# Two column pairs of the MLP's first product as 2x2x2 blocks of seven products

## The chip, the cores and the metric

The kernel runs on one core of one Trainium2 chip. The metric is the device time of one launch in microseconds (us), the median of several runs. TensorE is PE in the profile, with its weight loads as PEld; VectorE is DVE, ScalarE is ACT, GpSimd is POOL. SyncE (SP) issues most of the DMAs.

## What is computed

The reference is one transformer-like block on x of 2048 tokens by 512 channels, all in float32: a linear attention, then an MLP across the token axis.

```python
h = x + _A_ref(_layernorm(x, axis=-1), A_wqkv, A_w_phi, A_wo)
h2 = h + _B_ref(_layernorm(h, axis=-1), B_w1, B_b1, B_w2, B_b2)
```

Only the second line matters for the change. `_B_ref` normalizes its input once more and computes

```python
u = jnp.einsum("bsd,sf->bdf", h, w1) + b1                  # (B, D, F)
u = _gelu(u)
y = jnp.einsum("bdf,fs->bds", u, w2) + b2                  # (B, D, S)
```

with S = 2048, D = 512 and F = 1792. The first product multiplies W1 (2048 x 1792, transposed) with the normalized h (2048 x 512); the second multiplies W2 with the result u.

## The kernel before

**Three matmuls for one.** TensorE works in the type `float32r`. Every operand is split into a high part, a rounded copy, and a low part, the rest: the helper `split` (L56 to L59) has ACT write the high part and DVE or POOL subtract it. A product is then hi x hi + hi x lo + lo x hi: three matmuls (`mm3`, L61 to L65), added up in PSUM.

**The attention stage** ends at about 263 us. In it every engine's order is written out by hand (`tc.manual_schedule`, closed at L709). For each of the 16 token tiles t it forms h (`s_h`, L570), writes it to the output tensor `out` (L575), computes its mean and reciprocal deviation r2 (`s_moments`, `s_rstd`) and the normalized h, split into the tile `HN[t]` of 128 x 2 x 512 (`s_hn`, L587: two ACT operations, then the split with POOL as the subtracting engine). The 16 tiles HN stay in SBUF in the pool `big`, which has 18 places.

**The first product** (from L763) runs over seven column pairs p of W1, each 2 x 128 columns. For a pair, `fill` (L629) goes over the 16 token tiles: each time two blocks of 128 x 128 weights against the whole HN[t], 512 columns wide, three matmuls each, into two PSUM banks. W1 comes in chunks of two token tiles (`stream`, L612): one DMA of 256 KB on SP, an ACT copy to whi (L603), a DVE subtraction to wlo (L610); the pool `wf` holds four chunks. Pairs 0 and 1 run for the most part inside the attention stage, where TensorE has room for them; pairs 2 to 6 follow. After a pair, ACT applies the gelu from PSUM into a tile `u` (L738, pool `ur`, four places).

**The second product** already works in blocks of seven products. Take two operands as 2 x 2 blocks; seven products of sums of blocks (Winograd's form) take the place of eight. `operands_u` (L741) forms the block sums of u, with four subtractions of 128 x 256 by POOL for pairs 0 and 1 and by DVE for pairs 2 to 6, and splits all seven. Pairs 0 and 1 go to tiles of their own (`near`), pairs 2 to 6 into places of `big` that HN leaves. `stream_w2` (L779) loads blocks of W2 (two steps at a time, 256 KB each), sums them in four DVE operations (L789 to L792) and splits them; `products` (L803) issues the 7 x 3 = 21 matmuls of a step, 256 columns wide (L801). There are 8 row pairs with 7 steps each. At the end of a row pair `e`, `u2` and `u3` put the seven results together, and the rows are added to `out` by an accumulating DMA.

**The order.** After L709 a planner in the compiler orders the instructions of each engine: by the order in which the program issues them, by what is ready in its own timing model, and with pools handing out places as they come free. On the chip each engine then goes through its list in order. `tc.issue_after(x)` keeps what is issued inside it behind the instruction x on its engine; W2's sums use it, with an entry of `LO`, the list of W1's wlo subtractions.

Of the kernel before, what the change touches and what calls it, by code (L numbers as in the profile page):

```python
# [9 lines left out]
F32 = mybir.dt.float32  # L10
F32R = mybir.dt.float32r
AF = mybir.ActivationFunctionType
# [5 lines left out]
P = 128  # L18
S, D, H, DH, F = 2048, 512, 32, 16, 1792
NT = S // P  # L20
# [14 lines left out]
def block_kernel(ctx: ExitStack, tc: tile.TileContext, x, xT, wT, phic, wo, w1, b1, w2, b2,  # L35
                 kvmask, ident_in, out):
    nc = tc.nc

    cst = ctx.enter_context(tc.tile_pool(name="cst", bufs=1))
# [11 lines left out]
    cst.tile([P, 80], F32, name="pad")  # L51
# [4 lines left out]
    def split(hi, lo, src, lo_engine):  # L56

        nc.scalar.activation(hi, src, AF.Copy)  # L58
        lo_engine.tensor_sub(lo, src, hi)  # L59
# [452 lines left out]
    wst = ExitStack()  # L512
# [5 lines left out]
    HN, HT, PHT, OS, PO, VE = {}, {}, {}, {}, {}, {}  # L518
# [68 lines left out]
    def s_hn(t):  # L587
        hn = ak.tile([P, D], F32, name="hn")
        nc.scalar.activation(VE[t][:, 1:2], VE[t][:, 1:2], AF.Copy, scale=r2[:, t:t + 1])
        nc.scalar.activation(hn, HT[t], AF.Identity, scale=r2[:, t:t + 1], bias=VE[t][:, 1:2])  # L590
        HN[t] = big.tile([P, 2, D], F32R, name="hs", tag="big")
        split(HN[t][:, 0], HN[t][:, 1], hn, nc.gpsimd)
# [128 lines left out]

    NP = NF // 2
    HD = D // 2
    up = ctx.enter_context(tc.tile_pool(name="up", bufs=1, side="right", reuse_waits="tile"))
    uo = ctx.enter_context(tc.tile_pool(name="uo", bufs=2, side="right", reuse_waits="tile"))
    ws = ctx.enter_context(tc.tile_pool(name="ws", bufs=2, side="right", reuse_waits="tile"))
    ur = ctx.enter_context(tc.tile_pool(name="ur", bufs=4, side="right", reuse_waits="tile"))
    ut = ctx.enter_context(tc.tile_pool(name="ut", bufs=1, side="right", reuse_waits="tile"))
    ps_b = ctx.enter_context(tc.tile_pool(name="ps_b", bufs=4, space=PSUM, reuse_waits="tile"))
    NEAR = 2  # L730
    near = [up.tile([P, 7, 2, HD], F32R, name=f"un{p}") for p in range(NEAR)]
    up.tile([P, 120], F32, name="pad")
    U, UB, far = {}, {}, {}

    def gelu(f, pu):
        if f % 2 == 0:
            U[f // 2] = ur.tile([P, 4, HD], F32, name="u")
        nc.scalar.activation(U[f // 2][:, f % 2 * 2:f % 2 * 2 + 2].rearrange("p k d -> p (k d)"), pu,  # L738
                             AF.Gelu_apprx_tanh, bias=b1s[:, f:f + 1])

    def operands_u(p):  # L741
        u = U[p]
        tt = ut.tile([P, 3, HD], F32, name="tt")
        e = nc.gpsimd if p < NEAR else nc.vector
        e.tensor_sub(tt[:, 0], u[:, 0], u[:, 1])
        e.tensor_sub(u[:, 0], u[:, 2], u[:, 0])
        e.tensor_sub(tt[:, 1], u[:, 2], tt[:, 0])
        e.tensor_sub(tt[:, 2], u[:, 3], tt[:, 1])
        if p < NEAR:
            for n0, src in ((0, u), (4, tt)):  # L750
                o = near[p][:, n0:n0 + src.shape[1]]
                split(o[:, :, 0], o[:, :, 1], src, nc.vector)
            for m in range(7):
                UB[p, m] = near[p][:, m]
            return
        for m in range(7):
            at = (p - NEAR) * 7 + m
# [5 lines left out]
    for p in range(NP):  # L763
        while FN[p] < NT:
            fill(p, ps_b)
        for c in range(2):
            gelu(2 * p + c, PU[p][c])
        if p < NEAR:
            operands_u(p)
    for p in range(NEAR, NP):  # L770
        operands_u(p)
# [7 lines left out]
    def stream_w2(n):  # L779
        steps = STEPS[n:n + GRP]  # L780
        raw = ws.tile([P, GRP, 7, P], F32, name="wraw", bufs=3)
        wh_ = ws.tile([P, GRP, 7, P], F32R, name="whi")
        wl_ = ws.tile([P, GRP, 7, P], F32R, name="wlo")
        for i, (sp, p) in enumerate(steps):
            nc.sync.dma_start(raw[:, i, 0:4].rearrange("p (k i) s -> p k (i s)", k=2),
                              w2v[:, 2 * p:2 * p + 2, sp * 2 * P:(sp + 1) * 2 * P])
            AW[sp, p] = wh_[:, i], wl_[:, i]
        with tc.issue_after(LO[-18]):
            nc.vector.tensor_add(raw[:, :, 4], raw[:, :, 0], raw[:, :, 2])  # L789
            nc.vector.tensor_sub(raw[:, :, 0], raw[:, :, 1], raw[:, :, 0])  # L790
            nc.vector.tensor_sub(raw[:, :, 5], raw[:, :, 4], raw[:, :, 1])
            nc.vector.tensor_sub(raw[:, :, 6], raw[:, :, 3], raw[:, :, 5])  # L792
        split(wh_, wl_, raw, nc.vector)


    PROD = ((1, 1, 0, 0, True), (2, 6, 2, 1, True), (3, 3, 3, 1, True), (4, 4, 2, 0, False), (0, 0, 1, 0, True),
            (5, 5, 0, 1, False), (6, 2, 3, 0, False))

    def product(o, a, b, start, stop):
        for i, (x, y) in enumerate(((0, 0), (0, 1), (1, 0))):  # L800
            nc.tensor.matmul(o, a[x], b[:, y], start=start and i == 0, stop=stop and i == 2, skip_group_check=True)  # L801

    def products(sp, ps, order):  # L803
        for a, b, bk, half, opens in order:
            for p in ps:
                wh_, wl_ = AW[sp, p]
                product(bank[bk][:, half], (wh_[:, a], wl_[:, a]), UB[p, b], p == 0 and opens, p == NP - 1)

    def flat(a):
        return a.rearrange("p k d -> p (k d)")  # L810

    for n, (sp, p) in enumerate(STEPS):
# [4 lines left out]
        if p == 0:  # L817
            pools = [ps_f, ps_f, ps_q, ps_q] if sp % 2 else [ps_b] * 4
            bank = [pool.tile([P, 2, HD], F32, name="py", tag="pu") for pool in pools]
        if p < NP - 1 - 2 * last:  # L820
            products(sp, [p], PROD)
            continue
# [3 lines left out]
        e = uo.tile([P, 2, HD], F32, name="e")  # L826
        u2 = uo.tile([P, HD], F32, name="u2", bufs=1)
        u3 = uo.tile([P, HD], F32, name="u3")
        if not last:
            products(sp, [p], by_bank)  # L830
            ot = uo.tile([P, 2, 2, HD], F32, name="ot", bufs=1)
            nc.scalar.activation(e[:, 1], bank[0][:, 0], AF.Copy)
            nc.vector.tensor_add(u2, bank[0][:, 1], e[:, 1])
            nc.vector.tensor_add(u3, bank[1][:, 0], u2)
            nc.vector.tensor_add(e[:, 0], bank[2][:, 0], u2)
            for i, add in enumerate((u3.unsqueeze(1).to_broadcast([P, 2, HD]), e)):
# [9 lines left out]
        products(sp, [p - 2, p - 1, p], by_bank)  # L846
# [60 lines left out]
```

## Time and profile before

| | us |
|---|---|
| Median of 3 runs | 525.74 (525.53 to 526.3) |
| The profiled execution | 526.04 |
| Its span in the profile | 524.3 |
| PE busy in the span | 517.7 (99%) |
| DVE, ACT, POOL busy | 384.5, 277.8, 229.4 |
| Second product, first to last matmul | 378.6 to about 518 |

Times in the rows are microseconds from the start of the span. A row of the timeline has the start, the duration, the engine, the line, the operation, out<-in, the shape, and in brackets the idle time before it with what ended it. A row of a group has a count, then busy time and the mean in ns, then the idle time before the group's instructions with what ended that. Durations of neighbours on one engine can overlap by some 0.1 us (matmuls by more), so the distance between starts is what an instruction costs.

### The profile page before, as it was taken

What the parts mean: (1) busy time and instruction counts of PE and PEld (TensorE: products, weight loads), DVE (VectorE), ACT (ScalarE), POOL (GpSimd) and SP (SyncE); (2) the same over time, 40 slices, a digit from 0 to 9 for tenths busy, and PEclk for the clock granted to TensorE, in tenths of its full rate; (3) what the DMA queues carried; (4) which work ended last, traced back from release to release, by engine and by line L of the source; (5) the groups of instructions that cost most, each with busy time, mean ns of one, the idle gap of its engine ahead of it and who ended that gap; (6) DMA issues with size and microseconds to landing.
All of it is one profiled execution on the core that took longest, in us unless ns stands there. A gap on an engine that the chain in (4) does not pass through costs nothing.

```text
span 524.3 us, 10150 instructions
## 1 busy us (share of the span) xinstructions
PE 517.7 (99%) x4000; PEld 446.6 (85%) x4000; DVE 384.5 (73%) x681; ACT 277.8 (53%) x475; POOL 229.4 (44%) x174
## 2 busy tenths in 40 slices
PE   8999999999999999999999999999999999999996
PEld 7888888887877777777788888888899999999996
DVE  6893999986997899697336425726668878888774
ACT  6999853434267877767756433426544333343330
POOL 2579698985989999974224000000001101101110
PEclk9999999999999999999999999999999999999999
DMA  8643210021303333333255432532015556535631
GB/s 304 198 132 121 75 47 22 1 83 60 103 21 101 102 101 108 115 101 123 81 173 154 115 101 81 181 102 80 20 41 122 144 139 154 126 123 133 150 71 50
DMA packets 45487, 55.85 MB, mean 107 GB/s; under 512 B 3968, under 2 KB 33024, under 8 KB 45440
## 3 DMA queue, kind: packets, MB, share of 16 engines
q1 hardware_dynamic: 43136, 51.38, 30.9%
q0 software_dynamic: 2016, 3.67, 5.3%
q8 instruction: 31, 0.51, 0.4%
q10 hardware_dynamic: 288, 0.17, 0.1%
q14 instruction: 16, 0.13, 0.1%
HBM read 46.81 MB, written 8.39 MB: 105 GB/s over the span
## 4 chain that ended last, share of the span: by engine, by line
PE 95%; DVE 3%; ACT 1%; issue 0%; DVEq 0%; ACTq 0%
PE py L801 26%; PE pu L63 13%; PE pu L64 12%; PE pu L65 12%; PE pv L64 3%; PE pv L65 3%; PE po L63 3%; PE pv L63 3%; PE po L65 3%; PE po L64 3%; PE pk_ps L63 2%; PE pk_ps L65 2%; PE pk_ps L64 2%; PE pn L549 2%; PE tr L531 2%; PE kvp L208 2%
## 5 line engine op out<-in xcount | busy, mean ns | idle before, releaser
L839 POOL DMA_DIRECT2D out<-ot x14 | 12.4, 996 | 210.9 <-DVE ot L837 210.9
L801 PE MATMUL py<-uf,whi 128*128 128x256 f32 x560 | 96.2, 283 | 0.0
L58 ACT ACTIVATE whi<-wraw 128x1792 fp32r<-128x1792 f32 x28 | 47.7, 1704 | 77.9 <-PE py L801 73.8
L63 PE MATMUL pu<-hs,whi 128*128 128x512 f32 x224 | 87.7, 394 | 0.0
L64 PE MATMUL pu<-hs,whi 128*128 128x512 f32 x224 | 87.2, 389 | 0.0
L65 PE MATMUL pu<-hs,wlo 128*128 128x512 f32 x224 | 86.7, 389 | 0.0
L801 PEld LDWEIGHTS py<-uf,whi 128*128 128x128 f32 x560 | 83.3, 192 | 0.0
L610 DVE TENSOR_TENSOR wlo<-wraw,whi 128x512 fp32r<-128x512 f32 x56 | 47.3, 847 | 44.7 <-ACT whi L603 44.5
L59 DVE TENSOR_TENSOR wlo<-wraw,whi 128x1792 fp32r<-128x1792 f32 x28 | 56.6, 2022 | 18.6 <-ACT whi L58 18.6
L801 PE MATMUL py<-uf,wlo 128*128 128x256 f32 x280 | 69.9, 283 | 0.0
L603 ACT ACTIVATE whi<-wraw 128x512 fp32r<-128x512 f32 x56 | 34.6, 625 | 45.0 <-PE pu L64 40.8
L63 PEld LDWEIGHTS pu<-hs,whi 128*128 128x128 f32 x224 | 42.0, 188 | 9.1 <-ACT hj L581 0.2
L801 PEld LDWEIGHTS py<-uf,wlo 128*128 128x128 f32 x280 | 49.7, 192 | 0.0
L65 PEld LDWEIGHTS pu<-hs,wlo 128*128 128x128 f32 x224 | 42.0, 188 | 8.9
L64 PEld LDWEIGHTS pu<-hs,whi 128*128 128x128 f32 x224 | 42.1, 188 | 8.5
L443 POOL TENSOR_TENSOR ez<-eq,zB 128x1024 f32<-128x1024 f32 x16 | 38.5, 2408 | 4.4 <-ACT zB L487 4.4
L801 PE MATMUL py<-un,whi 128*128 128x256 f32 x224 | 38.4, 283 | 0.0
L196 POOL TENSOR_TENSOR pk<-pk,sk 128x1024 f32<-128x1024 f32 x16 | 31.0, 1941 | 7.7 <-DVE sk L195 5.4
L467 POOL TENSOR_TENSOR eq<-eq,w 128x1024 f32<-128x1024 f32 x16 | 32.4, 2025 | 3.2 <-DVE w L464 3.2
L801 PEld LDWEIGHTS py<-un,whi 128*128 128x128 f32 x224 | 33.2, 192 | 0.1
L200 POOL TENSOR_TENSOR zacc<-zacc,pk 128x1024 f32<-128x1024 f32 x13 | 31.2, 2404 | 0.5
L172 ACT ACTIVATE pk<-pk,r 128x1024 f32<-128x1024 f32 x16 | 18.4, 1147 | 17.9 <-DVE pk L150 17.7
(172 smaller groups left out, 1174.6 us busy)
## 6 DMA issues: line engine op xcount, KB each, us to landing
wraw<-in_w SPq DMA_DIRECT2D x112, 256.0 KB, 2.9
xraw<-in_xT SPq DMA_DIRECT2D x16, 256.0 KB, 3.1
xh<-in_x SPq DMA_DIRECT2D x16, 256.0 KB, 2.6
h<-in_x SPq DMA_DIRECT2D x16, 256.0 KB, 2.7
out<-h SPq DMA_DIRECT2D x16, 256.0 KB, 2.0
out<-ot POOLq DMA_DIRECT2D x14, 256.0 KB, 4.7
wraw<-in_wT SPq DMA_DIRECT2D x12, 256.0 KB, 5.1
wo<-in_wo SPq DMA_DIRECT2D x4, 256.0 KB, 3.8
```

Source lines behind the costliest of these rows:

```text
L58: nc.scalar.activation(hi, src, AF.Copy)
L59: lo_engine.tensor_sub(lo, src, hi)
L63: nc.tensor.matmul(o, ah, bh, start=first, stop=False)
L64: nc.tensor.matmul(o, ah, bl, start=False, stop=False)
L65: nc.tensor.matmul(o, al, bh, start=False, stop=last)
L196: nc.gpsimd.tensor_mul(heads(PK[t]), heads(PK[t]), sk.unsqueeze(2).to_broadcast([P, 2 * H, DH]))
L200: nc.gpsimd.tensor_add(zacc, zacc, PK[t])
L443: nc.gpsimd.tensor_mul(EZ[t], EQ[t], zB)
L467: nc.gpsimd.tensor_mul(heads(EQ[t]), heads(EQ[t]), W[t].rearrange("p g c h -> p (g c h)").unsqueeze(2).to_broadcast([P, 2 * H, DH]))
L603: nc.scalar.activation(wh_, raw, AF.Copy)
L610: LO.append(nc.vector.tensor_sub(wl_, raw, wh_).ins)
L801: nc.tensor.matmul(o, a[x], b[:, y], start=start and i == 0, stop=stop and i == 2, skip_group_check=True)
```

## The change

In the first product, column pairs 3 and 4 are computed like the second product. Each is 8 steps j, over two token tiles at a time. A step takes a 2 x 2 block of W1 (256 tokens by 256 columns) and a 2 x 2 block of the normalized h (256 tokens by 512 channels), and issues 7 x 3 matmuls of 256 columns. The other five pairs stay as they were. In the program's order pair 2 comes first, then 3, 4, 5 and 6.

- **h's block sums** (`sums_h`). HN holds only split parts. So the tiles of h are read back from `out` by 16 DMAs on SP into places of the pool `ur`, which u shares; normalized again on ACT, two operations of 128 x 512 a step, with r2 and a stored mean term `m2`; summed by POOL, four subtractions of 128 x 256 a step; and split into `TS[j]` by ACT and DVE (128 x 1024). ACT's and POOL's parts stand behind the last HN (`LASTH`). Three of the seven operands are halves of HN and need nothing. TS serves both pairs. Steps 0 and 1 are issued ahead of what is left of pairs 0 and 1, steps 2 to 7 between the fills of pair 2.
- **W1's blocks** (`blocks`, the former body of `stream_w2`): a DMA of 256 KB, four sums of 128 x 128, by DVE for pair 3 and by POOL for pair 4, and the split by ACT and DVE (128 x 896). Buffers: three raw, three whi, two wlo, laid over the memory of the pool `wf`, which is closed after pair 2 and opened again after pair 4.
- **The result** of such a pair is put together by `partial_sums` (the former e, u2, u3) and two DVE additions into `u`; the gelu then works in place.
- **Memory**: the tiles TS lie where W2's buffers (`ws`) and pair 1's operands (`near[1]`) lay. Both are opened only after pair 4, so W2's first loads and `operands_u(1)` move behind it. W2's first sums stand behind another entry of `LO`. `ot` goes to the pool `hp`.

The core of the diff:

```diff
     def s_hn(t):
...
-        nc.scalar.activation(VE[t][:, 1:2], VE[t][:, 1:2], AF.Copy, scale=r2[:, t:t + 1])
-        nc.scalar.activation(hn, HT[t], AF.Identity, scale=r2[:, t:t + 1], bias=VE[t][:, 1:2])
+        nc.scalar.activation(m2[:, t:t + 1], VE[t][:, 1:2], AF.Copy, scale=r2[:, t:t + 1])
+        nc.scalar.activation(hn, HT[t], AF.Identity, scale=r2[:, t:t + 1], bias=m2[:, t:t + 1])
...
-        split(HN[t][:, 0], HN[t][:, 1], hn, nc.gpsimd)
+        LASTH[:] = [nc.scalar.activation(HN[t][:, 0], hn, AF.Copy).ins,
+                    nc.gpsimd.tensor_sub(HN[t][:, 1], hn, HN[t][:, 0]).ins]
...
+    STRASSEN = (3, 4)
...
+    TS = {j: tp.tile([P, 4, 2, HD], F32R, name=f"ts{j}") for j in (7, 6, 5, 4, 3, 0, 1, 2)}
...
+    def sums(e, b12, b11, b22, b21, t1, t2, t3, t4):
+        e.tensor_sub(t1, b12, b11)
+        e.tensor_sub(t3, b22, b12)
+        e.tensor_sub(t2, b22, t1)
+        e.tensor_sub(t4, b21, t2)
+
+    def sums_h(j):
+
+        raw = ur.tile([P, 4, HD], F32, name="u")
+        for t in (2 * j, 2 * j + 1):
+            at = raw[:, 2 - 2 * (t % 2):4 - 2 * (t % 2)].rearrange("p k d -> p (k d)")
+            nc.sync.dma_start(at, out[t * P:(t + 1) * P, :])
+            with tc.issue_after(LASTH[0]):
+                nc.scalar.activation(at, at, AF.Identity, scale=r2[:, t:t + 1], bias=m2[:, t:t + 1])
+        with tc.issue_after(LASTH[1]):
+            sums(nc.gpsimd, raw[:, 2], raw[:, 3], raw[:, 0], raw[:, 1], raw[:, 3], raw[:, 0], raw[:, 2], raw[:, 1])
+        ts = TS[j]
+        split(ts[:, :, 0], ts[:, :, 1], raw, nc.vector)
+        HB[j] = [ts[:, 2], HN[2 * j][:, :, HD:D], HN[2 * j + 1][:, :, 0:HD], HN[2 * j + 1][:, :, HD:D],
+                 ts[:, 3], ts[:, 0], ts[:, 1]]
...
+    def blocks(raw, wh_, wl_, srcs, e, after=None):
+
+        for i, src in enumerate(srcs):
+            nc.sync.dma_start(raw[:, i, 0:4].rearrange("p (k i) s -> p k (i s)", k=2), src)
+        with (tc.issue_after(after) if after is not None else ExitStack()):
+            e.tensor_add(raw[:, :, 4], raw[:, :, 0], raw[:, :, 2])
+            e.tensor_sub(raw[:, :, 0], raw[:, :, 1], raw[:, :, 0])
+            e.tensor_sub(raw[:, :, 5], raw[:, :, 4], raw[:, :, 1])
+            e.tensor_sub(raw[:, :, 6], raw[:, :, 3], raw[:, :, 5])
+        split(wh_, wl_, raw, nc.vector)
+        return [(wh_[:, i], wl_[:, i]) for i in range(len(srcs))]
...
+    def plain(p, pool):
         while FN[p] < NT:
-            fill(p, ps_b)
+            fill(p, pool)
+            if p == STRASSEN[0] - 1 and len(HB) < NJ and FN[p] % 2 == 0:
+                sums_h(len(HB))
+        U[p] = ur.tile([P, 4, HD], F32, name="u")
         for c in range(2):
             gelu(2 * p + c, PU[p][c])
...
+    for j in range(2):
+        sums_h(j)
+    for p in range(STRASSEN[0]):
+        plain(p, ps_b)
+        if p in near:
             operands_u(p)
-    for p in range(NEAR, NP):
+    wst.close()
+    wst = ExitStack()
+    w1s = wst.enter_context(tc.tile_pool(name="w1s", bufs=1, reuse_waits="tile"))
+
+    W1 = {name: w1s.tile([P, 1, 7, P], F32 if name < "wha" else F32R, name=name)
+          for name in ("raw1", "raw0", "wlo0", "raw2", "whi1", "whi2", "wlo1", "whi0")}
+    for i, p in enumerate(STRASSEN):
+        bank = new_banks(i + 1)
+        for j in range(NJ):
+            n = i * NJ + j
+            w, = blocks(W1[f"raw{n % 3}"], W1[f"whi{n % 3}"], W1[f"wlo{n % 2}"],
+                        [w1v[:, 2 * j:2 * j + 2, p * 2 * P:(p + 1) * 2 * P]],
+                        nc.gpsimd if i else nc.vector)
+            products([(w, HB[j], j == 0, j == NJ - 1)], PROD)
+        rows = partial_sums()
+        U[p] = ur.tile([P, 4, HD], F32, name="u")
+        for c in range(2):
+            nc.vector.tensor_add(U[p][:, 2 * c:2 * c + 2], bank[2 + c], rows[c])
+            gelu(2 * p + c, None)
+    wst.close()
+    tst.close()
+    wst = ExitStack()
+    wf = wst.enter_context(tc.tile_pool(name="wf", bufs=4, reuse_waits="tile"))
+    un = ctx.enter_context(tc.tile_pool(name="un", bufs=1, side="right", reuse_waits="tile"))
+    near[1] = un.tile([P, 7, 2, HD], F32R, name="un1")
+    ws = ctx.enter_context(tc.tile_pool(name="ws", bufs=2, side="right", reuse_waits="tile"))
+    operands_u(1)
+    plain(5, ps_f)
+    plain(6, ps_q)
+    for p in range(2, NP):
         operands_u(p)
```

`new_banks`, `products` and `partial_sums` hold what stood in the second product's loop, and `stream_w2` now calls `blocks` with DVE as the summing engine.

More of the change, by code (lines that the diff above doesn't have):

```diff
@@ L729, in block_kernel @@
     ps_b = ctx.enter_context(tc.tile_pool(name="ps_b", bufs=4, space=PSUM, reuse_waits="tile"))
-    NEAR = 2
-    near = [up.tile([P, 7, 2, HD], F32R, name=f"un{p}") for p in range(NEAR)]
+    near = {0: up.tile([P, 7, 2, HD], F32R, name="un0")}
     up.tile([P, 120], F32, name="pad")
[L733 to L739, printed above, removed]
+    U, UB, HB, far = {}, {}, {}, {}
@@ L779, in stream_w2, with step @@
     def stream_w2(n):
[L780 to L810, printed above, removed]
+        group = STEPS[n:n + GRP]
+        tiles = [ws.tile([P, GRP, 7, P], dt, name=name, bufs=bufs)
+                 for name, dt, bufs in (("wraw", F32, 3), ("whi", F32R, 2), ("wlo", F32R, 2))]
+        AW.update(zip(group, blocks(*tiles, [w2v[:, 2 * b:2 * b + 2, a * 2 * P:(a + 1) * 2 * P] for a, b in group],
+                                    nc.vector, LO[-16])))
+    def step(sp, p):
+        return AW[sp, p], [UB[p, m] for m in range(7)], p == 0, p == NP - 1
     for n, (sp, p) in enumerate(STEPS):
@@ L817, in block_kernel @@
         if p == 0:
[L818 to L819 removed]
+            bank = new_banks(sp)
         if p < NP - 1 - 2 * last:
[L821 removed]
+            products([step(sp, p)], PROD)
             continue
```

65 lines of the change are left out of this document (42 added, 23 removed).

## The prediction, as it stands on record

> **What bounds the kernel now.** I read the totals first, then the chain, then two stretches by window.
>
> ```profile
> PE 517.7 (99%) x4000; PEld 446.6 (85%) x4000; DVE 384.5 (73%) x681; ACT 277.8 (53%) x475; POOL 229.4 (44%) x174
> ...
> PE 95%; DVE 3%; ACT 1%; issue 0%; DVEq 0%; ACTq 0%
> ```
> ```profile
> 263.00:292.00 29.00, 29.00 (x129) 24.02 (x128) 13.49 (x19) 16.84 (x28) 8.70 (x10) 1.00 0.55 168
> 292.00:378.00 86.00, 86.00 (x381) 71.19 (x380) 45.73 (x95) 34.60 (x66) 0.00 (x0) 1.00 0.33 97
> ```
>
> The window columns are PE, PEld, DVE, ACT and POOL busy, granted clock, DMA share and GB/s. TensorE is never idle from 263 to 378, the rest of the first product, and 95% of the chain is TensorE. A matmul less there is time less, as long as TensorE is fed. Durations overlap, so the price of a matmul is its pitch, from the timeline of PE:
>
> ```profile
> 375.67 0.39 PE L65 MATMUL pu<-hs,wlo 128*128 128x512 f32 x1
> ...
> 378.39 0.39 PE L65 MATMUL pu<-hs,wlo 128*128 128x512 f32 x1
> 378.62 0.40 PE L801 MATMUL py<-un,whi 128*128 128x256 f32 x2
> ...
> 383.65 0.40 PE L801 MATMUL py<-uf,whi 128*128 128x256 f32 x2
> ```
>
> From 375.67 to 378.39 lie 12 steps of 512 columns, 0.2267 us each. From 378.62 to 383.65 run 42 matmuls of 256 columns (two column pairs of the block product), 0.120 each. Two of 256 cost 0.240, 6% more than one of 512.
>
> **The gain.** A plain pair is 16 x 2 x 3 = 96 matmuls: 96 x 0.2267 = 21.76 us. A block pair is 8 steps of 7 x 3 = 21: 168 x 0.120 = 20.16 us, 2.52 a step. Two pairs save 2 x 1.60 = **3.2 us**. The seven-for-eight saving is half eaten by the shorter matmul.
>
> The Trainium skill ("TensorE: Matmul & The Clock Gate", Back-to-back issue gap) has 262 cycles for 256 columns and 518 for 512 at 2.4 GHz, 109 and 216 ns. By that the saving would be an estimated 2 x (20.7 - 18.3) = 4.8 us; the rows above decide for 3.2.
>
> **What feeding it costs.** Where do the stages lie? Pair 2, plain in both kernels, ends at 378.62 - 4 x 21.76 = 291.58; without waits the first block pair then runs to 311.74, and its step j (0 to 7) starts at 291.58 + 2.52 j. Before step j, h's tiles 2j and 2j+1 must be read back, normalized (ACT, two), summed (POOL, four of 128x256), and split (ACT copy, DVE subtraction, 128x1024); W1's block must be summed (DVE, four of 128x128) and split (ACT, DVE, 128x896). Nothing of the h work may start on ACT and POOL before the last tile of normalized h is done there:
>
> ```profile
> 268.63 1.29 POOL L59 TENSOR_TENSOR hs<-hn,hs 128x512 fp32r<-128x512 f32 x1 [1.92 <-ACT hs L58]
> ```
>
> That is 269.9. From there to step 7 (309.2) are 39.3 us. Engine by engine:
>
> ```profile
> L590 ACT ACTIVATE hn<-h,ve,r 128x512 f32<-128x512 f32 x16 | 13.1, 816 | 0.5
> L58 ACT ACTIVATE un<-u 128x1024 fp32r<-128x1024 f32 x2 | 2.1, 1067 | 2.3 <-POOL u L746 2.3
> L738 ACT ACTIVATE u<-pu,b1s 128x512 f32<-128x512 f32 x14 | 9.5, 687 | 10.0 <-PE pu L65 9.9
> L746 POOL TENSOR_TENSOR u<-u 128x256 f32<-128x256 f32 x2 | 1.5, 740 | 0.5 <-ACT u L738 0.4
> ```
>
> ACT: 8 x (2 x 0.82 + 1.07) = 21.7 for h, 8 x 0.94 = 7.5 for W1's blocks (the 128x1024 row x 896 / 1024), and about 10 for pair 2's last copies, six gelus and pair 0's split: 39.2, just inside the 40.6 that ACT has (POOL's row starts as ACT's part ends, 268.6). POOL: 9 x 4 x 0.74 = 26.6 (h, and pair 0's operands). Each fits by itself. But POOL and DVE do not run side by side here:
>
> ```profile
> L610 DVE TENSOR_TENSOR wlo<-wraw,whi 128x512 fp32r<-128x512 f32 x29 | 20.0, 692 | 34.2 <-ACT whi L603 34.0
> ```
> ```profile
> L610 DVE TENSOR_TENSOR wlo<-wraw,whi 128x512 fp32r<-128x512 f32 x15 | 18.7, 1248 | 0.0
> ```
> ```profile
> 243.20 1.94 POOL L467 TENSOR_TENSOR eq<-eq,w 128x1024 f32<-128x1024 f32 x1 [0.48 <-DVE w L464]
> ...
> 277.06 0.75 POOL L747 TENSOR_TENSOR tt<-u,tt 128x256 f32<-128x256 f32 x1
> 277.90 1.07 POOL L748 TENSOR_TENSOR tt<-u,tt 128x256 f32<-128x256 f32 x1
> ...
> 281.68 1.12 POOL L745 TENSOR_TENSOR tt<-u 128x256 f32<-128x256 f32 x1 [2.71 <-DVE un L59]
> ```
> ```profile
> 243.59 2.11 DVE L610 TENSOR_TENSOR wlo<-wraw,whi 128x512 fp32r<-128x512 f32 x1
> ...
> 270.46 0.69 DVE L610 TENSOR_TENSOR wlo<-wraw,whi 128x512 fp32r<-128x512 f32 x1 [4.15 <-ACT whi L603]
> ...
> 277.37 0.99 DVE L610 TENSOR_TENSOR wlo<-wraw,whi 128x512 fp32r<-128x512 f32 x1 [0.87 <-ACT whi L603]
> ...
> 281.52 0.68 DVE L610 TENSOR_TENSOR wlo<-wraw,whi 128x512 fp32r<-128x512 f32 x1
> ```
>
> The same subtraction of two SBUF operands takes 692 ns from 292 to 378, where POOL is at 0.00, and 1248 from 145 to 262 (first and second row). One by one: POOL's L467 ends at 245.14, DVE's L610, begun inside it, at 245.70, 0.56 later; L747 ends at 277.81, L610 at 278.36, 0.55 later; then the roles change, L610 ends at 278.36 and POOL's L748 0.61 later, and after the L610 of 281.52 POOL's L745 again 0.60 later. Whoever comes second waits until the first is done and then takes a fixed time: 0.55 for DVE's 128x512, **0.60 for POOL's 128x256**. For other lengths DVE's is scaled by
>
> ```profile
> L59 DVE TENSOR_TENSOR wlo<-wraw,whi 128x1792 fp32r<-128x1792 f32 x28 | 56.6, 2022 | 18.6 <-ACT whi L58 18.6
> L790 DVE TENSOR_TENSOR wraw<-wraw 128x256 f32<-128x256 f32 x28 | 11.8, 421 | 0.6
> ```
>
> (2022 - 692) / 1280 = 1.04 ns an element: 1.08 for 128x1024, 0.95 for 128x896, 0.82 for 128x768, 0.15 for 128x128. So in the 39.3 us must fit, one after the other:
>
> - pair 2's last six subtractions (270.46 to 281.52): 6 x 0.55 = 3.3;
> - pair 0's operands: 4 x 0.60 + 1.08 + 0.82 = 4.3;
> - eight steps of 4 x 0.60 + 1.08 + 4 x 0.15 + 0.95 = 5.03: 40.2.
>
> Together 47.8, to 317.7. With 0.3 for two hand-overs and the last step's 2.52 the pair ends at 320.5 and not 311.74: **8.8 us late** with never a pause. Pauses will be there (a u buffer goes round through DMA, ACT, POOL, ACT, DVE; four are shared, and pair 1's gelu holds one throughout; subtractions of wlo wait for TensorE to give back one of two buffers): 0 to 20% of 47.8, I take **2.6**. Queued behind a waiting h subtraction on DVE are W1's own, behind a waiting normalization on ACT W1's copies, behind an h read on SP W1's loads; TensorE waits for all of these.
>
> The upper end is the same list by whole durations (0.74 for POOL, 0.69, 1.22, 1.09 and 0.29 for DVE): 61 us, 13 more. The Trainium skill ("SBUF — State Buffer", SBUF: two separate sides) says that VectorE with two SBUF inputs and GpSimd exclude each other "for the whole instruction", which would be this upper end; the three hand-overs above show less.
>
> Second block pair: the sums go to POOL as 128x128. No row has that; 128x256 bounds it with 0.60 from above and, by elements, with the half from below. 4 x 0.30 to 0.60 plus 0.95 gives 2.2 to 3.4 a step against 2.52. One of three raw buffers goes round in 2.9 (load) + about 2.4 + 0.94 + 1.09 + 0.6 = 7.9, 2.6 a step. Cost 0 to 6; with one or two steps' lead I take **1.0**.
>
> ```profile
> wraw<-in_w SPq DMA_DIRECT2D x112, 256.0 KB, 2.9
> hb<-out SPq DMA_DIRECT2D x2, 256.0 KB, 2.7
> ```
>
> At nothing: the 16 reads of h (4.2 MB; six loads of W2 leave the same stretch, whose DMA share is 0.55; if a load is late it is 2.7 to 2.9). W2's buffers open only after the second block pair: the six loads, sums and splits lie under pairs 5 and 6 (43.5 us). Pair 1's operands move there too. The partial sums lie beside the next pair, which has other banks. Without that cover each is 3 to 6 us.
>
> **Sum.** On the profiled execution (526.04, span 524.3): -3.2 + 8.8 + 2.6 + 1.0 = +9.2, 535.2. It stood 0.3 over the median of 525.74, so **534.9 us**.
>
> **Rivals.**
> - *The two engines get by each other* (faster). If the exclusion falls in pauses, or holds less of the short POOL operations than the three hand-overs suggest, ACT's 39.2 us still fit, nothing waits, and 525.74 - 3.2 = 522.5 stands. It decides where the serial list is under 42 us (39.3 plus the gain); that needs 0.44 in place of 0.60 for POOL's 36 operations. Against it: three hand-overs within 0.01, and 1248 against 692.
> - *It nearly cancels*: waits of 2 to 4 us, 526. Only if the list is 42 us.
> - *TensorE slows down when it rests, or the buffers run in turn.* A matmul of the same 128x128 shape took 430 ns at the kernel's start against 272 later:
>
> ```profile
> L289 PE MATMUL pk_ps<-ones 128*128 128x128 f32 x18 | 4.2, 430 | 1.1 <-DVE eps L54 1.1
> L272 PE MATMUL pv<-ident,wraw 128*128 128x128 f32 x8 | 1.0, 272 | 0.0
> ```
>
>   At 1.6 times, a step takes 4.0; two to four such steps behind the last wait and at the start of the second pair give 3 to 6 us, and whole durations in the serial list 13 more: 538 to 554, 547 as one number. The clock is granted at 1.00 in every window above, but TensorE never rests in them. The Trainium skill ("TensorE: Matmul & The Clock Gate", What's actually happening) halves the clock after an idle window of some 3.4 us; no run here shows that yet.
>
> **How the numbers follow.** Forecast (serial list, 529 to 543) 0.72; both side by side 0.14; cancelled 0.05; worse than 543 0.09. A measurement of this kernel tells about 0.2% from no change, 1 us. Faster 0.14, same 0.05, slower 0.81. The range leaves out the faster case and the last half of the worst: 525 to 546.
>
> **What would show it.** The gain: PE pitch 0.120 in block pairs. The exclusion: between 270 and 320 DVE subtractions of 128x1024 well over 1.22 and POOL's 128x256 well over 0.74 on average, and waits of TensorE in the first block pair, released by DVE (ts or wlo), of about 11 us in all; few in the second; none in pairs 5 and 6 or the second product. It is wrong if POOL's operations stay at 0.74, if TensorE is busy throughout 292 to 312, if the waits name DMA, or if they lie elsewhere.

## The result and the profile after

| | before | after |
|---|---|---|
| Median of 5 runs, us | 525.86 (525.53 to 526.36) | 549.06 (548.3 to 549.28) |
| Profiled execution, its span | 526.04, 524.3 | 549.28, 547.5 |
| PE busy in the span | 517.7 (99%) | 521.4 (95%) |

The ratio is 1.0435 (95% interval 1.042 to 1.0451): the change costs 23.2 us. The direction was forecast, the size was not: 549 lies above the range of 525 to 546.

The page's rows of PE and of its clock (one digit for each fortieth of the span, 13.7 us) show at once that something new is there: between 287 and 301 us PE is busy for less than 40% of the time, and behind that the clock is not full.

```profile
PE   8999999999999999999993699799999999999996
...
PEclk9999999999999999999998599989999999999999
```

By window (columns as in the prediction):

```profile
263.00:292.00 29.00, 29.00 (x129) 23.74 (x127) 12.88 (x15) 22.34 (x34) 22.07 (x25) 1.00 0.48 145
292.00:315.00 23.00, 8.98 (x49) 8.62 (x49) 16.50 (x26) 13.81 (x19) 17.56 (x19) 0.63 0.39 126
...
340.00:360.00 20.00, 15.61 (x106) 14.47 (x107) 11.77 (x17) 9.59 (x13) 7.80 (x13) 0.93 0.42 127
```

PE loses 14 us in 292 to 315 and 4.4 in 340 to 360; in both its clock is below 1.00. Right behind the first of these rests, from 305.2 to 312, the granted clock is 0.50, and matmuls of 256 columns follow each other at 0.21 us instead of 0.120 (two of them from 308.97 to 309.40 in the timeline below). This is called half clock from here on. The waits of PE from 263 to 402, all there are (us in total, times, longest):

```profile
PE py L802 <- ACT whi L59: 13.6, 2, 13.0
PE pu L64 <- ACT whi L605: 4.3, 1, 4.3
PE py L802 <- DVE wlo L60: 1.0, 1, 1.0
```

Forecast were waits of about 11 us inside the first block pair, released by DVE, and none in pairs 5 and 6. What came is one long wait ahead of the block pair, for W1's first block, 1.0 inside it that DVE released, and one wait ahead of pair 5. By the prediction's own sign ("if they lie elsewhere") it is wrong there. The timeline of PE gives the borders:

```profile
291.68 0.39 PE L66 MATMUL pu<-hs,wlo 128*128 128x512 f32 x1
305.10 0.80 PE L802 MATMUL py<-hs,whi 128*128 128x256 f32 x2 [13.03 <-ACT whi L59]
...
308.97 0.63 PE L802 MATMUL py<-ts,whi 128*128 128x256 f32 x2
309.40 0.63 PE L802 MATMUL py<-ts,wlo 128*128 128x256 f32 x2
...
322.26 0.40 PE L802 MATMUL py<-hs,whi 128*128 128x256 f32 x2
...
324.78 0.40 PE L802 MATMUL py<-hs,whi 128*128 128x256 f32 x2
...
329.95 0.50 PE L802 MATMUL py<-hs,whi 128*128 128x256 f32 x2
...
352.06 0.28 PE L802 MATMUL py<-hs,wlo 128*128 128x256 f32 x1
356.65 0.50 PE L64 MATMUL pu<-hs,whi 128*128 128x512 f32 x1 [4.31 <-ACT whi L605]
...
401.88 0.40 PE L802 MATMUL py<-un,whi 128*128 128x256 f32 x2
```

The borders are the starts: 291.91 (the last `pu` at 291.68 plus its 0.23), 329.95 (the second block pair begins), 352.18, and 401.88 (the second product, 378.62 before).

| us | forecast | measured | off |
|---|---|---|---|
| to the end of pair 2 | 291.58 | 291.91 | +0.3 |
| first block pair, its wait included | 31.6 | 38.04 | +6.5 |
| second block pair | 21.2 | 22.23 | +1.1 |
| pairs 5 and 6, their wait included | 43.5 | 49.70 | +6.2 |

Forecast: 20.16 + 8.8 + 2.6, 20.16 + 1.0, 2 x 21.76. The four differences make 14.1 of the 14.2 between 534.9 and 549.06. The gain is there as forecast: step to step is 2.52 us (322.26 to 324.78, 21 matmuls of 0.120) where nothing waits.

What holds W1's first block back? SP's queue (start, then the time from the first to the last issue of the group):

```profile
278.45 15.86 SPq L756 DMA_DIRECT2D u<-out  x8
294.36 1.45 SPq L787 DMA_DIRECT2D raw<-in_w  x3
```

Eight reads of h take 15.86 us to be issued, because SP waits for a place in `ur` to come free, and what frees it is the subtraction that ends a `ts` (SP's waits from 262 to 360, then the chain of work):

```profile
SPq L756 <- DVE ts L60: 19.4, 4, 8.9
```
```profile
292.14 1.35 DVE ts L60
...
293.51 0.33 SPq L756
...
294.36 4.08 DMA raw<-in_w
...
298.53 0.29 DVE raw L789
298.82 1.14 DVE ts L60
...
303.49 0.20 DVE raw L792
```

W1's first load is the next in the queue. It lands at 298.4. Its four sums are dealt out on DVE among `ts` subtractions and the sums of later blocks; the last of them, L792, is the row of 303.49. ACT's copy follows at 304.11, and TensorE starts at 305.1. The exclusion of POOL and DVE that the prediction worked with is there as well:

```profile
292.14 1.34 DVE L60 TENSOR_TENSOR ts<-u,ts 128x1024 fp32r<-128x1024 f32 x1 [5.91 <-ACT ts L59]
...
298.74 1.22 DVE L60 TENSOR_TENSOR ts<-u,ts 128x1024 fp32r<-128x1024 f32 x1
```
```profile
292.36 1.70 POOL L749 TENSOR_TENSOR tt<-u,tt 128x256 f32<-128x256 f32 x1
...
298.90 1.64 POOL L747 TENSOR_TENSOR u<-u 128x256 f32<-128x256 f32 x1 [0.75 <-ACT u L758]
```

Both times POOL's 0.74 becomes 1.6 to 1.7, and it ends 0.58 after DVE's subtraction: the 0.60 of the prediction. The averages from 270 to 320 are as forecast too: 1.39 for DVE's `ts` subtractions (1.21 to 1.77) and 0.97 for POOL's sums.

Did the end of the list set the end of the pair? No:

```profile
317.94 1.21 DVE L60 TENSOR_TENSOR ts<-u,ts 128x1024 fp32r<-128x1024 f32 x1
```

This is the last `ts`. It is done at 319.15, when TensorE is at the end of the fourth of its eight steps (the fifth begins at 319.52). From there on h's blocks were all ready, and the pair ended at 329.95 because it had begun at 305.10 and at half clock.

On the exclusion itself: the Trainium skill ("SBUF — State Buffer", SBUF: two separate sides) has the second one wait for the whole of the first; the traces show that less than its own full duration is left after that (0.58 of 0.74).

### The profile page after: what moved, and what is told of

It reads as the page before. It is cut to its first block, busy times and chain, and to the rows that moved or that the text cites. A ratio compares the mean times of both kernels' runs of the same rounds, so it can differ in the third digit from the quotient of the medians.

```text
span 547.5 us, 10649 instructions
## 1 busy us (share of the span) xinstructions
PE 521.4 (95%) x4144; PEld 455.1 (83%) x4144; DVE 418.1 (76%) x731; ACT 303.0 (55%) x501; POOL 280.1 (51%) x238
## 4 chain that ended last, share of the span: by engine, by line
PE 81%; DVE 7%; DMA 4%; POOL 3%; ACT 3%; issue 2%; SPq 0%; DVEq 0%; POOLq 0%; ACTq 0%
PE py L802 27%; PE pu L64 9%; PE pu L65 8%; PE pu L66 8%; PE pv L65 3%; PE pv L66 3%; PE po L64 3%; PE pv L64 3%; PE po L66 3%; PE po L65 2%; PE pk_ps L64 2%; DMA raw<-in_w 2%; PE pk_ps L65 2%; PE pk_ps L66 2%; PE pn L550 2%; PE tr L532 2%
## 5 line engine op out<-in xcount | busy, mean ns | idle before, releaser
L64 PE MATMUL pu<-hs,whi 128*128 128x512 f32 x160 | 63.5, 400 | 4.3 <-ACT whi L605 4.3
L65 PE MATMUL pu<-hs,whi 128*128 128x512 f32 x160 | 62.9, 393 | 0.0
L66 PE MATMUL pu<-hs,wlo 128*128 128x512 f32 x160 | 61.6, 394 | 0.0
L612 DVE TENSOR_TENSOR wlo<-wraw,whi 128x512 fp32r<-128x512 f32 x40 | 36.0, 907 | 11.2 <-DMA wraw<-in_w 5.6
L64 PEld LDWEIGHTS pu<-hs,whi 128*128 128x128 f32 x160 | 30.3, 189 | 11.3 <-ACT whi L605 4.5
L66 PEld LDWEIGHTS pu<-hs,wlo 128*128 128x128 f32 x160 | 30.5, 190 | 6.5
L65 PEld LDWEIGHTS pu<-hs,whi 128*128 128x128 f32 x160 | 30.5, 190 | 6.0
L802 PE MATMUL py<-hs,whi 128*128 128x256 f32 x96 | 20.3, 301 | 13.6 <-ACT whi L59 13.6
L605 ACT ACTIVATE whi<-wraw 128x512 fp32r<-128x512 f32 x40 | 24.5, 622 | 13.1 <-PE pu L65 5.5
```

Source lines behind the costliest of these rows:

```text
L64: nc.tensor.matmul(o, ah, bh, start=first, stop=False)
L65: nc.tensor.matmul(o, ah, bl, start=False, stop=False)
L66: nc.tensor.matmul(o, al, bh, start=False, stop=last)
L605: nc.scalar.activation(wh_, raw, AF.Copy)
L612: LO.append(nc.vector.tensor_sub(wl_, raw, wh_).ins)
```

## The experiments

Two theories stood against each other at first. **A**: the order of SP's queue (W1's first loads behind reads of h that wait for places, and a load of W2 ahead of pair 5's) makes both waits, and TensorE's half clock behind them costs the rest. **B**, the prediction's: POOL and DVE, which work one at a time, set the end of the first block pair, whatever the order. All medians are compared with the kernel before on the same chip (525.7 to 526.4).

| kernel | median us | ratio to before (95%) | first block pair ends |
|---|---|---|---|
| after | 549.06 | 1.0435 (1.042 to 1.0451) | 329.95 |
| h's sums on DVE | 545.2 | 1.037 (1.0351 to 1.0388) | 328.13 |
| W1's loads first | 548.95 | 1.0429 (1.0413 to 1.0446) | 329.09 |
| both of these | 541.65 | 1.0293 (1.0277 to 1.0308) | 321.00 |
| W2's loads behind | 549.52 | 1.0447 (1.0432 to 1.0463) | 329.75 |
| pair 5 first | 543.25 | 1.0326 (1.0309 to 1.0343) | 329.77 |
| added matmuls | 552.68 | 1.0502 (1.0485 to 1.052) | not compared |
| all four edits | 535.17 | 1.0172 (1.0157 to 1.0187) | 321.25 |
| ... h's work let ahead | 535.61 | 1.0181 (1.0164 to 1.0198) | 320.76 |
| ... all sums on DVE | 534.47 | 1.0155 (1.0137 to 1.0172) | 320.17 |
| ... and handover in order | 534.62 | 1.0162 (1.0146 to 1.0177) | 322.44 |
| one block pair | 530.47 | 1.0077 (1.0061 to 1.0094) | |
| ... handover in order | 528.21 | 1.0043 (1.003 to 1.0055) | |
| ... third place | 526.39 | 1.001 (1.0001 to 1.0019) | |

**h's block sums on DVE.**

```diff
-            sums(nc.gpsimd, raw[:, 2], raw[:, 3], ...)
+            sums(nc.vector, raw[:, 2], raw[:, 3], ...)
```

> h's block sums go from POOL to DVE (32 subtractions of 128x256 at 0.42 us each, the mean of DVE's own 128x256 row, 13.4 us more on DVE), everything else as after. So POOL has nearly nothing left to do between 270 and 320, and POOL and DVE can't keep each other from SBUF there. B (the serial list of POOL and DVE sets the end of the first block pair): the list shrinks by 32 x (0.60 - 0.42) = 5.8 us at the least, and with POOL's blocking gone DVE's own subtractions run back to back; the first block pair ends 6 to 9 us earlier and the time is 540 to 543. A (SP's order: the first W1 block loads stand behind reads of h that wait for places, issued at 294.4): the loads come earlier only by as much as the places come free earlier, some 1 to 3 us, so the time is 545 to 549, and the wait ahead of the first block pair is still 9 us or more, with the issue of the first block load of W1 still behind 290.

PE's waits and SP's queue:

```profile
PE py L802 <- ACT whi L59: 13.0, 1, 13.0
```
```profile
279.82 15.12 SPq L756 DMA_DIRECT2D u<-out  x10
294.99 45.01 SPq L787 DMA_DIRECT2D raw<-in_w  x16
```

545.2, which is A's number: the wait is as long as ever, and W1's first load is again issued as soon as the reads are (295.0). But inside the pair no wait is left, so POOL and DVE no longer set its end here. With the start unmoved, the pair still ends at 328.

**W1's first three loads ahead of the reads for steps 5 to 7.**

```diff
+    for n in range(3):
+        ahead = load(W1[f"raw{n}"], [...])
+    with tc.issue_after(ahead):
+        while len(HB) < NJ:
+            sums_h(len(HB))
```

> The first three block loads of W1 are issued on SP ahead of the reads of h for steps 5 to 7, which wait for places; arithmetic and engines as after. A (SP's order): the first block pair starts where pair 2 ends, at about 292, the 13.2 us wait goes, and so does the half clock after it (3.3 us); what is left is the last tile of h's sums, ready at 319.2 in the run of the change, so that the pair ends at about 322 and not at 330: -8 us, 541 (538 to 544). B (the serial list alone): the order of the loads tells nothing, since the last h sums end the pair either way: 547 to 551, with the wait moved from in front of the pair into it.

548.95 is B's number: the order on SP alone is not the whole cause. The pair starts 5.8 earlier (299.34), and ends 0.9 earlier. The waits are only moved:

```profile
PE py L806 <- ACT whi L59: 11.6, 4, 7.9
...
PE py L806 <- DVE wlo L60: 2.4, 3, 1.3
```
```profile
299.26 2.34 SPq L756 DMA_DIRECT2D u<-out  x4
301.81 11.38 SPq L785 DMA_DIRECT2D raw<-in_w  x4
313.95 0.82 SPq L756 DMA_DIRECT2D u<-out  x2
```

Now the last read of h stands behind four loads of W1, which wait for their buffers, and the last `ts` comes at 324.0 instead of 317.9. Here, in one queue, whichever goes first holds up the other.

**Both edits.**

> Both edits at once: h's block sums on DVE, and W1's first three block loads ahead of the reads of h for steps 5 to 7. With the sums on DVE alone the first block pair ran without a wait from 305.2 to 328.1, but began 13.4 us late. A (only the order on SP): now it begins where pair 2 ends, at about 292, with no rest and no half clock: 545.2 - 13.2 - 2.7 = 529. A serial list under it (what is left of the prediction's B): DVE's own work from 270 on, by the distances of starts in the run with the sums on DVE, is 32 x 0.335 (h sums) + 8 x 1.14 (ts) + 32 x 0.205 and 8 x 1.0 (W1) + 6 x 0.6 (pair 2) + 4.0 (pair 0 and 1's operands), and POOL's eight operations hold it up 8 x 0.6: 46.8 us, to 316.6, and with the last step 319 for the end of the pair in place of 328: 545.2 - 9 = 536 (534 to 538), with waits inside the pair released by DVE or by ACT behind DVE.

541.65, 3.5 less than with the sums on DVE alone, where 9 were expected from the list and 16 from the order. The pair starts at 296.24 and ends at 321.00 (the list had 319), 7.1 earlier; 1.8 of that is given back in the second block pair, which took 21.0 behind the late pair and 22.8 here. That leaves 5.2, the difference of the two spans (545.2 and 540.0); the profiled execution with the sums on DVE was the longest of its four, 1.8 over their median, which is why the medians differ by less. So there are two bounds nested in one another: while W1's loads stand behind the reads, the order on SP gives the start, and DVE's list gives an end of about 320, which nothing below moves.

Why does neither kernel start the pair at 292? W1's first load is issued at 285.65 and 286.45, but on DVE its sums stand behind a subtraction of `uf` (pair 2's operands). With W1's loads first alone, DVE waits there for ACT, which comes to this operand behind pair 2's gelu:

```profile
294.56 0.53 DVE L60 TENSOR_TENSOR uf<-u,uf 128x256 fp32r<-128x256 f32 x1 [1.70 <-ACT uf L59]
```

W1's first sum follows at 295.02. With both edits DVE is busy with h's sums and `ts` until 293.4, and W1's first sum runs at 293.99. Once W1's loads are ahead, the start is set on DVE as well.

**W2's loads behind pair 5's fourth.**

```diff
+        with (tc.issue_after(LD[-13]) if after is not None else ExitStack()):
             for i, src in enumerate(srcs):
                 nc.sync.dma_start(...)
```

`LD` is the list of W1's plain loads.

> The first loads of W2, one of which stood on SP at 352.0 ahead of all loads of pair 5, waiting for memory that opens only as pair 4 ends, are issued behind pair 5's fourth load; nothing else changes. A: the wait of 4.5 us ahead of pair 5 goes, and the half clock after it (1.7 us) too, less at most 1 us for what W2's later loads cost at the start of the second product: -5 to -6.2, 543 to 544. B (the prediction, which put W2's loads at nothing and named waits only in the two block pairs): no change, 549.

549.52: no change, so the order on SP alone is not the whole cause here either. SP's queue in the kernel after, and then in this one:

```profile
352.01 0.37 SPq L787 DMA_DIRECT2D wraw<-in_w  x1
352.47 1.96 SPq L619 DMA_DIRECT2D wraw<-in_w  x4
```
```profile
345.22 6.51 SPq L619 DMA_DIRECT2D wraw<-in_w  x4
```

Pair 5's loads do go out 7 us earlier. TensorE's rest stays, in two pieces, and DVE's timeline shows why:

```profile
PE pu L64 <- ACT whi L605: 2.3, 1, 2.3
PE pu L66 <- DVE wlo L612: 1.7, 1, 1.7
```
```profile
352.32 0.42 DVE L821 TENSOR_TENSOR u<-py,e 128x256 f32<-128x256 f32 x1 [2.05 <-ACT e L820]
...
353.45 1.22 DVE L60 TENSOR_TENSOR un<-u,un 128x1024 fp32r<-128x1024 f32 x1
...
356.65 1.89 DVE L612 TENSOR_TENSOR wlo<-wraw,whi 128x512 fp32r<-128x512 f32 x3
```

Seven operations stand ahead of pair 5's first subtraction on DVE: pair 4's result and pair 1's operands, both of which the prediction had put beside pair 5 at no cost. In the kernel after, the two queues were ready at nearly the same time: ACT's first copy for pair 5 waited for its load until 355.96, and DVE, behind these seven, came to the first subtraction at 356.76.

**Pair 5 first.** As the last kernel, and those operations behind pair 5's third chunk on ACT and DVE.

```diff
+    for _ in range(8):
+        fill(5, ps_f)
+    finish(STRASSEN[1], HI[-2], LO[-2])
+    operands_u(1, HI[-2], LO[-2])
```

`HI` holds W1's copies as `LO` holds its subtractions; `finish` is `partial_sums` with the two additions and the gelu.

> W2's loads behind pair 5's fourth load, as before, and besides the putting together of pair 4's result and the split of pair 1's operands (ACT 0.4 + 1.0 + 0.8, DVE some 4.4) kept behind the third chunk of pair 5 on ACT and DVE; nothing else changes against the kernel after. If these stood in pair 5's way on ACT and DVE, the rest ahead of pair 5 shrinks from 4.6 to the copy and the subtraction of one chunk, 1.3 to 2.0, and, as rests up to 2.3 us cost no clock so far, the 2.0 of half clock behind it go too: -4.5 to -5.3, 544 to 545. If it is something else (the buffers' memory opens only with pair 4's last matmul and the loads come after that), the rest stays over 4 and the time at 549.

543.25, 5.8 less than after, a little over what was expected (4.5 to 5.3). This kernel has both mends, W2's loads and the order on ACT and DVE; no run has the second alone. PE has no wait at pair 5, and this window is full:

```profile
340.00:360.00 20.00, 20.00 (x132) 18.34 (x133) 11.05 (x15) 8.54 (x12) 7.68 (x13) 1.00 0.55 166
```

**Matmuls added in the long wait.** 54 of 512 columns, of which nothing is read.

> 54 matmuls of 512 columns whose results nothing reads (12 us at 0.2267) follow pair 2 and fill the 13.2 us in which TensorE waits for the first block; everything else as after. If TensorE's clock is halved because it rested, the first 36 or so matmuls of the block pair take 0.12 and not 0.21, and the time falls by up to 3.3 us, 545.7 to 547; the granted clock between 292 and 315 is near 1.00 in place of 0.63. If the slow start of the block pair is something else (operands that come late, the weights' way in), the matmuls stay at 0.21 and the time at 549, or above by what the added matmuls overrun. The later stages (pairs 5 and 6 at 356 with half the clock) stay as they are in either case.

552.68, slower by 3.6. It settles less than it should have: the planner dealt out DVE's sums in another order, the first block came at 306.69, 1.6 later, and TensorE rested 2.88 ahead of it. The slow stretch became shorter, 16 matmuls at 0.21 in place of 28, but the time went to waits inside the pair. Keeping TensorE busy was no use here, since the data were late.

**All four edits, and two variants.**

> All four edits together: h's sums on DVE, W1's first loads ahead, W2's loads and the rest of pair 4 and pair 1 behind pair 5's first chunks. The terms add up if they are separate: (the two edits at the first block pair, 529 or 536) - 5 = 524 by the order alone, 531 by the serial list. Before stands at 526.4, so only the first would be faster than before.

535.17: the forecast by the list was 531, by order alone 524. The pieces do add up (541.65 - 5.8 = 535.9), and 13.9 of the 14.2 us that the prediction was off are gone; that it lands on 534.9 is in part luck, since the forecast had h's sums on POOL. DVE is nearly full up to the pair's end:

```profile
292.00:315.00 23.00, 16.61 (x120) 16.02 (x121) 21.16 (x55) 14.05 (x19) 0.00 (x0) 0.93 0.44 139
```

The first variant takes out the two `issue_after(LASTH...)`:

> As the kernel with all four edits, but h's block work need not stand behind the last tile of the normalized h: four normalizations on ACT come ahead of its last two operations, and the first sums and splits of TS ahead on DVE. If a serial list from 270 on sets the end of the first block pair, it begins up to 3 us earlier and the time falls by 1 to 3 against the kernel with all four. If the last tile itself comes later by those 2 to 3 us of ACT, plain pair 2 could wait for it, but its last matmuls come 25 us later, so nothing is lost. If only the order on SP counts, no change.

535.61, no change. The first sums do come earlier, but the reads of h for steps 5 and 6 are issued at 292.1, as before (292.2): they wait for places, so the list begins earlier and gets a pause instead. The second has DVE do pair 4's and pair 1's sums:

```diff
-                        nc.gpsimd if i else nc.vector, loaded=n < 3)
+                        nc.vector, loaded=n < 3)
...
```

> As the kernel with all four edits, and POOL does nothing more between 270 and 400 but pair 0's operands: pair 4's sums of W1's blocks go to DVE, pair 1's four sums too, behind pair 5's third chunk. Second block pair: it took 22.9 against 20.16 with POOL's sums of 0.46 to 1.33 each in front of the copy; on DVE four take 0.8, so a raw buffer goes round in less and the pair takes 20.2 to 21: -2 to -2.7. First block pair: pair 1's sums held up DVE's list by some 2 us (0.96 in place of 0.42 three times, 1.23 in place of 0.69): -1 to -2. Together 535.2 - 3 to 5 = 530 to 532. If the rest of the loss is something else than the exclusion of POOL and DVE and DVE's list, 535.

534.47. The first block pair gains 1.1 (320.17), the second none: it took 23.25. So POOL's sums were not what holds up the second pair. I read it as a want of lead: the first pair uses up every block as it comes, and blocks go round in three buffers; no run shows that by itself.

**One block pair.** Pair 3 plain, pair 4 in blocks; h's work lies in 43.5 us.

```diff
-    STRASSEN = (3, 4)
+    STRASSEN = (4,)
...
-            if p == STRASSEN[0] - 1 and len(HB) <= 4 and FN[p] % 2 == 0:
+            if p in (2, 3) and len(HB) < NJ and FN[p] % 4 == 0:
```

> Only pair 4 runs in blocks of seven products; pair 3 is plain again. The edits at the order on SP, at pair 5's beginning and the sums on DVE are kept (W1's and pair 1's sums on DVE too), and h's reads, sums and splits are spread over the 43.5 us of the plain pairs 2 and 3. The gain of one pair is 1.6. If the gain is real and only the feeding cost was in the way (43.5 us against DVE's 19.8 for h and 19.2 for the chunks of the two pairs, and no queue in which a block load stands behind a read of h), the time is 526.0 - 1.6 = 524.4, with 0 to 2 us of rest where pair 3 hands over to pair 4: 524.4 to 526.4. If the blocks of seven cost something of their own that no order removes, the time is over 527.

530.47. No read of h holds anything up, but at the handover TensorE rests twice for 2.0 us and runs 15 matmuls at half clock: on DVE a sum of the third block, whose load waits for memory of pair 3's last chunk, stands ahead of the first block's subtraction, and on ACT pair 3's gelu ahead of the first copy. The next kernel turns these two round, and so does one with two block pairs:

```diff
+            if n == 1:
+                with tc.issue_after(BH[1]):
+                    gelus(p - 1)
```

`BH` and `BL` list the blocks' copies and subtractions; the third block's sums stand behind `BL[0]`.

> As the kernel with pair 4 alone in blocks, with the handover from pair 3 put in order: pair 3's gelu, which waits for the pair's last matmul, stands behind the copies of the first two blocks on ACT, and the sums of the third block, whose load waits for memory of pair 3's last chunk, behind the first block's subtraction on DVE. There TensorE rested twice for 2.0 us (313.5 and 316.5) and ran 15 matmuls at half clock, 1.6 us. If these two queues are the whole of what is left, 4 to 5.5 us go: 525.0 to 526.5, and the time is at or just under the kernel before (526.4), by at most the 1.6 of one pair less what rest remains. If a block pair costs something beyond what stands in the queues, it stays over 528.

> The same two edits on the kernel with two block pairs and all sums on DVE (534.5). There the rest ahead of the first block pair is 4.05 us and the half clock behind it 2.5. If the queues set this rest, both go and the time is 528 to 529. If DVE's own list from 270 on (40 to 43 us of distances of starts) sets the end of the first block pair, the rest only moves into the pair, where rests under 2.3 us cost no clock: 532 to 533.5, and the first block pair still ends at 318 to 320.

With one pair 528.21: the rest is one of 2.34 us ahead of step 2, where the third block arrives. With two pairs 534.62, no change, and both forecasts were missed: 528 to 529 if the queues set the rest, 532 to 533.5 and an end at 318 to 320 if DVE's list does. The first block pair now starts at 294.18, with a first rest of 2.2, and ends at 322.44. The rest moved into the pair, as the list would have it, but there it cost clock, which the expectation had ruled out for rests under 2.3:

```profile
301.61 0.51 PE L815 MATMUL py<-hs,whi 128*128 128x256 f32 x2 [1.97 <-ACT whi L805]
...
304.47 0.58 PE L815 MATMUL py<-hs,wlo 128*128 128x256 f32 x1 [1.64 <-DVE wlo L806]
```

Behind the second of these two waits 14 matmuls ran at half clock.

The last kernel gives the third block a free place of `ur`:

> As the one block pair with its handover in order, but the third block of W1 is loaded into a place of the pool that u and h share, which is free by then, and not into memory that pair 3's last chunk holds until its last matmul; the sums of blocks 4 and 5 stand behind the third block's subtraction on DVE. In the run before, the block pair took 23.3 us against 20.16 of matmuls: a rest of 2.34 ahead of step 2, and 0.65 in steps 0 and 1. If only the buffers' memory holds step 2 up, 1.8 to 2.3 go: 525.9 to 526.4, level with the kernel before (526.1), and fewer waits than 1 us in the block pair, which would then cost no more than the plain one (21.8). If the time does not fall, what holds step 2 up is not the memory of the load.

526.39 against 525.67, 0.1% above before, which is all of the loss that is left. From the first block matmul to the first of pair 5:

```profile
313.52 0.40 PE L815 MATMUL py<-hs,whi 128*128 128x256 f32 x2
...
335.70 0.50 PE L64 MATMUL pu<-hs,whi 128*128 128x512 f32 x1
```
```profile
PE py L815 <- DVE wlo L806: 1.1, 2, 0.7
```

22.18 us for a block pair, 21.76 for a plain one. With 2.0 us of waits and partial waits left, all of the 1.6 is used up. No kernel here is faster than the one before.

## Why the prediction was wrong in size

- **The gain** of 3.2 was right: 0.120 a matmul, 2.52 a step.
- **The exclusion of POOL and DVE** was right as a mechanism: 0.58 against 0.60 for POOL's 128x256, and 1.08 and 1.09 for DVE's 128x1024 behind POOL (277.34 to 278.42, 302.40 to 303.49), where 1.08 had been scaled from another length. (The text lists four hand-overs and calls them three; no number changes.) As what sets the end of the first block pair it was wrong in this kernel: h's part of the list was done at 319.15, within 317.7 plus 2.6, and the pair ended 10.8 later. Five kernels with the order mended end it at 320.2 to 322.4, near the 320.5 of the list. That is in part luck, since their list has the sums on DVE and adds up differently.
- **The step that failed is the pauses**, "0 to 20% of 47.8, I take 2.6". The text named the mechanism ("Queued ... behind an h read on SP W1's loads; TensorE waits for all of these") and then priced it as a share of the list. It is no share. Measured, the first block pair came 17.9 late (38.04 less 20.16) and not 8.8 + 2.6. The reads wait for `ur`, in which u holds places too, so the loads behind them come at a time of their own: 294.4, and 10.7 us of loading, sums and splitting later TensorE starts. Of the 17.9, 13.2 are the wait ahead, 2.9 half clock (28 matmuls at 0.21 and more instead of 0.12), and the rest small waits inside. 9.1 in place of 2.6 still lies inside the 20% allowed; it is the 2.6 that was too little, by 6.5, and the wait came ahead of the pair instead of within it.
- **"At nothing" failed at pair 5**: pair 1's operands and "The partial sums lie beside the next pair", with "Without that cover each is 3 to 6 us" as its price. TensorE's banks were free; ACT's and DVE's queues weren't, and on SP one of W2's loads stood ahead of pair 5's. That is 4.5 of rest and 1.7 of half clock, 6.2 in all; mending both gave 5.8. Either of the two errors alone would have left the time inside the range: 549.06 - 6.5 = 542.6 and 549.06 - 6.2 = 542.9.
- **W2's loads at nothing**: mending their place alone gave nothing (549.52), because the next queues were ready no earlier. That does not show that they cost nothing. How the 6.2 divide between SP's queue and those of ACT and DVE stays open.
- **The second block pair** was mis-sized by 1.1: 2.1 over 20.16, not 1.0. Its price was looked for in POOL's sums; moved to DVE they gave nothing.
- **The rival "TensorE slows down when it rests"** (538 to 554) holds the measured time; the case above 543 had a chance of 0.09. Its price for the slow matmuls was about right, 3 to 6 us; measured 4.6. Its place was not: it put them behind the last wait and at the start of the second pair, and they came behind the first wait, in steps 0 and 1 of the first block pair, and at pair 5. Its other 13 us, whole durations in the list, did not come, so that its 547 lies near 549 by luck. Half clock is not a case of its own: here it came with every rest of 2.9 us and more, so a forecast with rests has to carry it.

What stays open: in the second block pair, how the 2 to 3 us divide between the three buffers and the order of DVE's queue; no run took the buffers apart.

## What to carry to other kernels

A read that waited for a place held up all that stood behind it on SP's queue, so price a new wait by who comes next in that queue and when the place comes free, not as a percentage of the work. Where a stage hands over to another, look at the first operand of the next one on every queue it passes (load, copy, subtraction): mending SP's queue alone gave nothing here, at either handover, since the next queue was ready with the same wait. And count the gain against one handover first: 1.6 us a pair was less than the 2.0 of waits that remained after all these mends.

## What the runs showed of the hardware

At a granted clock of 0.50, TensorE's matmuls are step to step 0.21 apart for 256 columns and 0.43 for 512, against 0.120 and 0.227. The first matmuls of pair 5 in the kernel after, two at half clock and one at the full one:

```profile
357.27 0.63 PE L64 MATMUL pu<-hs,whi 128*128 128x512 f32 x1
357.69 0.63 PE L65 MATMUL pu<-hs,whi 128*128 128x512 f32 x1
...
360.62 0.39 PE L65 MATMUL pu<-hs,whi 128*128 128x512 f32 x1
```

Fifteen rests of 2.9 to 13.7 us were each followed by 3 to 8 us of it, at a cost of 1.4 to 3.0 us; single rests of up to 2.3 cost one slower matmul. Two rests close together are another matter: 2.0 and 2.0 with 0.9 of work between them cost 1.6 (one block pair), 2.25 and 1.92 with 0.9 cost 1.5 (two block pairs, handover in order), and 2.6 and 2.1 with 0.8 at pair 5 cost 1.6 (W2's loads behind), each time behind the second rest. The Trainium skill ("TensorE: Matmul & The Clock Gate", What's actually happening) has the clock halved after an idle window of about 3.4 us that runs freely; the 2.9 and the pair of 2.0 show that less rest than that, or rest in two pieces, is enough, and the prediction's "no run here shows that yet" is settled by these.

A POOL sum of 128x128, which the trace of before did not have, took 0.45 at its shortest and, beside DVE, 0.55 to 0.82 on average for the four sums of a block. The first of them:

```profile
L789 POOL TENSOR_TENSOR raw<-raw 128x128 f32<-128x128 f32 x8 | 5.0, 622 | 13.9 <-DMA raw<-in_w 13.9
```
